# RWKV-7 attention and SwiGLU block on one core: the early triangular inverses of two chunks made together on 128 partitions

## The chip, the core and the metric

The kernel runs on one core of a Trainium2 chip. The metric is device time in microseconds from the first to the last work of one execution; the number given for a kernel is the median of several runs. Names of engines: PE is TensorE (matrix products and transposes), DVE is VectorE, ACT is ScalarE, POOL is GpSimd, SP is SyncE, which here only issues transfers (DMAs).

## The reference

Two layers stand one behind the other. The first is a linear recurrence over 768 time steps for 4 x 8 = 32 independent sequences with a 40 x 40 state each:

```
for t in range(S):
    y[:, :, t] = einsum('bhd,bhde->bhe', rt, state)
    Sa = einsum('bhde,bhe->bhd', state, at)
    state = state * wt[:, :, None, :] - einsum('bhd,bhe->bhde', Sa, bt) + einsum('bhd,bhe->bhde', vt, kt)
```

The second takes y as 3072 tokens of 320 numbers, divides each by its root mean square, and computes `(silu(xn @ w_gate) * (xn @ w_val)) @ w_out` with 1536 hidden units. All is float32; the weights arrive as 8-byte numbers whose halves the kernel reads as integers and narrows to float32 itself.

## The kernel before, in words

**Chunks.** The recurrence is cut into 24 chunks of 32 steps. For a chunk c there are four stages. `front(c)` loads w, a, k, b and v, transposes them on PE, and builds by levels 1, 2, 4, 8, 16 the matrix of the products between the steps of the chunk: on each level ACT copies an operand (`KE`), PE multiplies ("gram"), and DVE copies the masked product into the tile `LT`. The last of the five masked copies completes `LT`. `early_inverse(c)` (chunks 0 to 3) or `inverse(c)` (the others) solves the unit lower triangular system of each sequence. `main(c)` uses the inverse, the state and the products for the output y of the chunk and the next state, and turns y to tokens, normalized, in the tile `xg`. After every second chunk `feed(g)` runs the SwiGLU layer for the 256 tokens of two chunks: products of 256 columns with the gate and value weights (`xg,w` in the profile), and the product with `w_out` into PSUM tile `po`. `narrow(f, h)` makes the float32 weights; all 24 of these are due before feed 0 ends.

**The early inverse.** Each sequence's 32 x 32 triangle is split into two 16 x 16 diagonal blocks and one block between. The diagonal blocks of the 32 sequences lie on 64 partitions: partition u*32+n has block u of sequence n. To get there, four DMAs write `LT` to the DRAM tile `sB`, and two read it back into the part B of tile `M`. Then DVE does 15 steps of two instructions on the part Y of `M`: a product into `tmp`, and a subtraction from Y. Each needs the one before. ACT makes the negative transpose of the upper block (line 783), three DMAs write Y to the DRAM tile `sY`, and eight read it back, turned to the layout of PE, into the part E of `M`, which lies over the place of B and Y. PE then does two sets of 32 small products ("inv", lines 793 and 797), each copied out of PSUM by ACT, and the full inverse stands in E. `main(c)` uses it in the second set of its products "lower" (line 822, written `Xs,M` in the profile). Chunk c uses buffer c mod 2 of `M`.

**Order.** Nothing is scheduled at run time. The program first lists all pieces of work in a plan, and then issues them in the order of a written table `ORDER`: each number picks a piece relative to the first that is not yet issued, and a "-" puts in one filler product on PE (line 1010) that computes nothing needed. A second table, `PAIRS`, gives each PSUM tile its bank. Each engine works strictly in this order, SP's and POOL's transfers too: an instruction that waits holds up all that stands behind it on its engine. PE uses the products of the feeds as filling between the short, dependent products of the chunks.

Every helper records its engine's operation, so nearly all DVE work has line 453, PE 495 (products) and 498 (transposes), ACT 476 and 479, DMAs 492. Names in the rows: `LT_102`, `LT_103`, `LT_104` belong to chunks 0, 1 and 2, `M_135` and `M_136` are the two buffers of `M`.

## Time and profile before

| | |
|---|---|
| median of the runs | 932.68 us (three runs, 931.99 to 933.84) |
| time of the profiled execution | 934.37 us |
| its span, first to last instruction | 932.6 us |
| PE, DVE, ACT, POOL busy | 875.7, 723.2, 521.9, 294.9 us |
| mean granted clock of PE | 0.991 |

The page of the profile gives totals. A table by windows gives, for a stretch of the span, how long each engine was busy, the granted clock and the share of the DMA engines. A timeline gives single instructions with their start and duration in microseconds; in brackets stands the idle time of the engine before it, and what ended that.

### The profile page before, as it was taken

The page shows a single profiled execution, that of the slowest core. Times are in us where ns is not written, and L with a number is a line of the kernel's source. Part 1 is how long each engine was busy: PE and PEld are TensorE (multiplying, and loading weights), DVE is VectorE, ACT ScalarE, POOL GpSimd, SP SyncE. Part 2 cuts the span into 40 slices and gives each one's busy share as a digit, 9 for nine tenths or more (in the row PEclk, how much of TensorE's full clock was granted, in tenths as well). Part 3 has the DMA queues.
Part 4 walks back from the last instruction along what each step waited for, and adds up shares of the span by engine and source line. Part 5 has one row for each costly group of instructions (what it writes and reads, how often), then busy time and mean ns, then how long its engine had stood idle before and what let it go on. Part 6 is the DMA issues. An engine that isn't in the chain of part 4 may idle for free.

```text
span 932.6 us, 50195 instructions
## 1 busy us (share of the span) xinstructions
PE 875.7 (94%) x22072; PEld 703.2 (75%) x22072; DVE 723.2 (78%) x2702; ACT 521.9 (56%) x1144; POOL 294.9 (32%) x515
## 2 busy tenths in 40 slices
PE   4776898899999999999999999999999999999998
PEld 4665776677777788777777887887787777878776
DVE  5887778878878888978888888888888887864511
ACT  5887877674555566565555655655545454432211
POOL 8576546404221323432221333412503320200000
PEclk9999999899999999999999999999999999999999
DMA  9653546223242243333323223413414222021000
GB/s 162 104 119 84 126 98 153 73 69 67 55 87 49 46 86 73 71 59 60 70 39 74 64 54 75 89 35 71 88 21 85 61 41 62 11 60 28 3 15 15
DMA packets 146363, 63.01 MB, mean 68 GB/s; under 512 B 128800, under 2 KB 138080, under 8 KB 146144
## 3 DMA queue, kind: packets, MB, share of 16 engines
q1 hardware_dynamic: 125664, 29.46, 17.1%
q0 software_dynamic: 18368, 30.01, 15.1%
q8 instruction: 173, 2.83, 1.3%
q10 hardware_dynamic: 2112, 0.33, 0.3%
q14 instruction: 46, 0.38, 0.1%
HBM read 49.15 MB, written 10.09 MB: 64 GB/s over the span
## 4 chain that ended last, share of the span: by engine, by line
PE 72%; DMA 9%; DVE 6%; ACT 6%; issue 3%; SPq 2%; POOL 1%; DVEq 0%; POOLq 0%; ACTq 0%
PE ps L495 50%; PE po L495 14%; PE ps L498 7%; SPq L492 2%; DMA M<-sB 2%; DMA w<-in_moe_w_out_dram 1%; DMA LT<-sY 1%; DMA w<-in_moe_w_gate_dram 1%; DVE tmp L453 1%; DVE y L453 1%; DMA sY<-Yi 1%; ACT VU L476 1%; ACT KE L476 1%; DVE Yi L453 1%; DMA sY<-M 1%
## 5 line engine op out<-in xcount | busy, mean ns | idle before, releaser
L495 PE MATMUL ps<-xg,w 128*128 128x256 f32 (+1 forms) x1728 | 354.2, 393 | 1.2 <-DVE Yi L453 0.5
L495 PEld LDWEIGHTS ps<-xg,w 128*128 128x128 f32 (+1 forms) x1728 | 263.7, 191 | 49.1 <-issue 12.4
L495 PE MATMUL po<-w,hT 128*128 128x320 f32 x576 | 179.0, 449 | 0.0
L492 POOL DMA_DIRECT2D VU<-in_v_dram x184 | 102.4, 560 | 172.7 <-PE ps L495 78.1
L453 DVE TENSOR_TENSOR tmp<-Yi,M 128x60 f32<-128x60 f32 (+24 forms) x620 | 129.3, 209 | 20.5 <-DMA M<-sB 6.1
L453 DVE TENSOR_TENSOR Yi<-Yi,tmp 128x60 f32<-128x60 f32 (+24 forms) x620 | 129.7, 210 | 13.8
L473 ACT ACTIVATE sg<-ps 128x256 f32<-128x256 f32 x144 | 52.6, 384 | 150.6 <-PE ps L495 143.1
L495 PEld LDWEIGHTS po<-w,hT 128*128 128x128 f32 x576 | 106.0, 192 | 37.4 <-issue 1.9
L476 ACT COPY KE<-K 128x512 f32<-128x512 f32 x168 | 110.6, 662 | 26.2 <-DVE K L453 18.2
L453 DVE TENSOR_TENSOR hT<-ps,sg 128x256 f32<-128x256 f32 x144 | 58.3, 420 | 68.7 <-ACT sg L473 57.4
L453 DVE TENSOR_TENSOR K<-K,T 128x256 f32<-128x256 f32 x240 | 98.9, 421 | 10.2 <-ACT KE L476 8.8
L495 PE MATMUL ps<-A,KE 40*64 40x72 f32 x3840 | 95.0, 247 | 9.0 <-ACT KE L476 1.7
L495 PEld LDWEIGHTS ps<-A,KE 40*64 40x64 f32 x3840 | 79.2, 149 | 28.9 <-issue 9.3
L476 ACT COPY KN<-ps 128x320 f32<-128x320 f32 x144 | 67.4, 471 | 59.1 <-PE ps L495 28.5
L453 DVE COPY_PREDICATED LT<-msk,ps 128x256 f32<-128x256 uint32 x120 | 65.9, 550 | 19.5 <-PE ps L495 10.2
L482 POOL TENSOR_TENSOR ss<-ss,mhalf 128x1 f32<-128x1 f32 x24 | 15.4, 641 | 194.2 <-DVE ss L453 179.2
L453 DVE TENSOR_TENSOR y<-y,ps 128x256 f32<-128x256 f32 x119 | 49.9, 419 | 11.0 <-PE ps L495 7.9
L453 DVE TENSOR_TENSOR A<-A,T 128x128 f32<-128x128 f32 (+1 forms) x168 | 55.8, 335 | 1.5 <-ACT A L476 0.4
L495 PEld LDWEIGHTS ps<-As,KN 64*40 64x40 f32 x3840 | 45.1, 123 | 12.7 <-issue 4.4
L495 PE MATMUL ps<-As,KN 64*40 64x32 f32 x3840 | 50.3, 204 | 3.1 <-DVE y L453 1.6
L476 ACT COPY VU<-ps 32x320 f32<-32x320 f32 x96 | 40.0, 417 | 15.5 <-PE ps L495 14.2
L492 POOL DMA_DIRECT2D wan<-in_w_dram x44 | 29.1, 661 | 57.4 <-PE ps L498 57.1
(121 smaller groups left out, 1250.2 us busy)
## 6 DMA issues: line engine op xcount, KB each, us to landing
M<-sB SPq DMA_DIRECT2D x80, 128.0 KB, 3.4
rn<-in_r_dram SPq DMA_DIRECT2D x24, 160.0 KB, 4.6
out_dram<-o SPq DMA_DIRECT2D x48, 80.0 KB, 2.3
VU<-in_v_dram POOLq DMA_DIRECT2D x184, 20.0 KB, 2.6
kbn<-in_b_dram POOLq DMA_DIRECT2D x44, 80.0 KB, 3.4
kbn<-in_k_dram POOLq DMA_DIRECT2D x44, 80.0 KB, 3.3
wan<-in_w_dram POOLq DMA_DIRECT2D x44, 80.0 KB, 3.1
wan<-in_a_dram POOLq DMA_DIRECT2D x44, 80.0 KB, 3.3
```

The source lines that it names most:

```text
L453: plan.add("DVE", kind, lambda at: fn(at(o), *m(at)), [o], aps(*args))
L473: plan.add("ACT", "act", lambda at: nc.scalar.activation(at(o), at(a), f, **kw), [o] + aps(acc), [a])
L476: plan.add("ACT", "copy", lambda at: nc.scalar.copy(at(o), at(a)), [o], [a])
L482: plan.add("POOL", "tt", lambda at: nc.gpsimd.tensor_tensor(o, a, b, op), [o], [a, b])
L492: plan.add(by, "dma", lambda at: queue.dma_start(out=o, in_=i), [o], [i])
L495: return o, lhsT, rhs, lambda at: nc.tensor.matmul(at(o), lhsT, rhs, start=start, stop=stop, skip_group_check=True)
L498: return o, i, ident, lambda at: nc.tensor.transpose(at(o), i, ident)
```

## The change

`early_inverse` is called only at chunks 1 and 3 and works for two chunks. The diagonal blocks of both lie in the M tile of the even chunk, on all 128 partitions: partition (2u+q)*32+n has block u of sequence n of the pair's chunk q. The 30 DVE instructions per inverse keep their number of elements per partition; there are two sets of them and no longer four. What follows, from the DMAs to `sY` on, is still done per chunk, each chunk's E in its own tile `M`.

```
-        return (f[0:2 * BH, 0:h * h].rearrange("p (s t) -> p s t", s=h),
-                f[0:2 * BH, h * h:3 * h * h].rearrange("p (s t) -> p s t", s=h),
+        return (f[:, 0:h * h].rearrange("p (s t) -> p s t", s=h),
+                f[:, h * h:3 * h * h].rearrange("p (s t) -> p s t", s=h),
...
-                dma(halves(M)[0][u * BH:(u + 1) * BH], sB.rearrange("n (s t) -> n s t", s=C)[:, (1 - u) * HC:(2 - u) * HC, u * HC:(u + 1) * HC])
+                dma(halves(Z[c - c % 2]["M"])[0][(2 * u + c % 2) * BH:(2 * u + c % 2 + 1) * BH], sB.rearrange("n (s t) -> n s t", s=C)[:, (1 - u) * HC:(2 - u) * HC, u * HC:(u + 1) * HC])
...
     def early_inverse(c):
-        z = Z[c]
         plan.stage = "inverse", c
-        LT = z["LT"]
-        B, Y, E, A = halves(z["M"])
+        B, Y, _, _ = halves(Z[c - 1]["M"])
...
         for i in range(HC - 1):
             n, m = i + 1, HC - 1 - i
-            tmp = tmp_.next()[0:2 * BH, 0:n * m].rearrange("p (s t) -> p s t", s=n)
-            tt(tmp, Y[:, 0:n, m:m + 1].to_broadcast((2 * BH, n, m)), ap(B, m * HC + HC - 1, (0, n), (-1, m)), MUL)
+            tmp = tmp_.next()[:, 0:n * m].rearrange("p (s t) -> p s t", s=n)
+            tt(tmp, Y[:, 0:n, m:m + 1].to_broadcast((P, n, m)), ap(B, m * HC + HC - 1, (0, n), (-1, m)), MUL)
             tt(Y[:, 0:n, 0:m], Y[:, 0:n, 0:m], tmp, SUB)
-        scale(Y[0:BH, :, HC:], Y[0:BH, :, 0:HC].rearrange("p s t -> p t s"), -1.0)
-        sY = sY_.next()[:, 0:3 * HC * HC].rearrange("n (s t) -> n s t", s=HC)
-        dma(sY[:, :, 0:HC], Y[0:BH, :, 0:HC])
-        dma(sY[:, :, HC:C], Y[BH:2 * BH, :, 0:HC])
-        dma(sY[:, :, C:], Y[0:BH, :, HC:])
-        blank(E[:, :, 0:C], 0.0)
...
+        scale(Y[0:2 * BH, :, HC:], Y[0:2 * BH, :, 0:HC].rearrange("p s t -> p t s"), -1.0)
+        held = []
+        for q in range(2):
+            sY = sY_.next()[:, 0:3 * HC * HC].rearrange("n (s t) -> n s t", s=HC)
+            dma(sY[:, :, 0:HC], Y[q * BH:(q + 1) * BH, :, 0:HC])
+            dma(sY[:, :, HC:C], Y[(2 + q) * BH:(3 + q) * BH, :, 0:HC])
+            dma(sY[:, :, C:], Y[q * BH:(q + 1) * BH, :, HC:])
+            held.append(sY)
+        for q in range(2):
+            z, sY = Z[c - 1 + q], held[q]
+            LT = z["LT"]
+            _, _, E, A = halves(z["M"])
+            blank(E[:, :, 0:C], 0.0)
...
             front(c + 2)
-            (early_inverse if c + 2 < EARLY else inverse)(c + 2)
+            if c + 2 >= EARLY:
+                inverse(c + 2)
+            elif c % 2:
+                early_inverse(c + 2)
```

What follows in the second loop (eight loads of E, two sets of products, two copies) is as before. The tables `ORDER` and `PAIRS` are written anew throughout; one line of the old table and one of the new:

```
-0 225 226 223 0 0 0
...
+1211 1101 1207 1208 1209 1117 1116 1210 453 1066 1119 1394 1392 1146 1118 1067 454 1068 1069 1199 1070 1142 1120 1071
```

The number of PE's pieces (929) and of SP's transfers (486) stays; DVE's pieces go from 2699 to 2639, ACT's from 1122 to 1120, POOL's from 506 to 502, and the filler products on PE from 28 to 32. The last 146 pieces on PE and the last 479 on DVE stand in the same order in both.

Where the rows now stand, at three places. On DVE, around the inverse of chunk 0 (`tmp` and `M_135`) and the last masked copies of chunk 1 (`COPY_PREDICATED LT_103`), before:

```order
L453 TENSOR_TENSOR K_129<-K_129,T_126 128x16x16
L453 TENSOR_TENSOR tmp_139<-M_135 64x55
L453 COPY_PREDICATED LT_103<-msk,ps_65 128x32x8
L453 TENSOR_TENSOR M_135<-M_135,tmp_139 64x5x11
L453 TENSOR_TENSOR tmp_140<-M_135 64x60
L453 TENSOR_TENSOR K_129<-K_129,T_126 128x16x16
L453 TENSOR_TENSOR M_135<-M_135,tmp_140 64x6x10
L453 TENSOR_TENSOR tmp_139<-M_135 64x63
```

and now, at the first step of the inverse of chunks 0 and 1:

```order
L450 TENSOR_TENSOR T_127<-T_127 128x128
L450 TENSOR_TENSOR T_127<-T_127 128x64
L450 SCALAR_TENSOR_TENSOR w_154<-w_162,ex_171 128x480
L450 TENSOR_TENSOR tmp_139<-M_135 128x15
L450 TENSOR_TENSOR M_135<-M_135,tmp_139 128x15
L450 TENSOR_TENSOR tmp_140<-M_135 128x28
L450 TENSOR_TENSOR M_135<-M_135,tmp_140 128x2x14
L450 TENSOR_TENSOR tmp_139<-M_135 128x39
```

The inverse of chunk 0 ran between the last masked copies of chunk 1; the joint one begins after all of them, after three weight slices (`w_154` is written twice ahead of it) and after the first instructions of chunk 2 (`T_127`).

On SP, the transfers around the same inverses, before:

```order
L492 DMA sB1_174<-LT1_103 32x8x32 x3
L492 DMA gcol_84<-in_moe_rms_g_dram 128x1
L492 DMA sB1_174<-LT1_103 32x8x32
L492 DMA sY0_175<-M0_135 32x16x16 x3
L492 DMA M1_136<-sB1_174 32x16x16 x2
L492 DMA M0_135<-sY0_175 16x8x16 x4
L492 DMA M0_135<-sY0_175 16x8x32 x4
```

and now:

```order
L489 DMA sB1_174<-LT1_103 32x8x32 x4
L489 DMA M0_135<-sB1_174 32x16x16 x2
L489 DMA rn0_97<-in_r_dram 64x16x40
L489 DMA gcol_84<-in_moe_rms_g_dram 64x1
L489 DMA sY0_175<-M0_135 32x16x16 x2
L489 DMA sY1_176<-M0_135 32x16x16 x3
L489 DMA sY0_175<-M0_135 32x16x16
L489 DMA gcol_84<-in_moe_rms_g_dram 64x1
L489 DMA M0_135<-sY0_175 16x8x16 x4
L489 DMA M0_135<-sY0_175 16x8x32 x4
L489 DMA M1_136<-sY1_176 16x8x16 x2
```

The six stores of both chunks to `sY` now stand together, ahead of the loads of chunk 0's E; the loads of chunk 1's E follow directly.

On PE, from the turning of chunk 0's output (`ident,y_146`) to the use of chunk 1's inverse (`Xs_143,M_136`), before:

```order
L498 MATMUL ps_63<-ident,y_146 128x40 x8
L495 MATMUL ps_64<-ST_101,aP_134 32x40 x32
L495 MATMUL ps_64<-VU_99,LT_103 32x40 x32
L498 MATMUL ps_65<-ident,ST_101 104x40 x16
L495 MATMUL ps_64<-A_131,KE 64x72 x16
L495 MATMUL ps_65<-M_136,LT_103 16x16 x32
L495 MATMUL ps_65<-M_136 32x16 x32
L495 MATMUL ps_63<-Xs_143,M_136 32x40 x32
```

and now:

```order
L495 MATMUL ps_64<-ident,y_146 128x40 x8
L495 MATMUL ps_65<-ident,KE 128x40 x16
L492 MATMUL ps_63<-VU_99,LT_103 32x40 x32
L492 MATMUL ps_65<-A_132,KE 64x72 x16
L492 MATMUL ps_63<-A_131,KE 64x72 x16
L492 MATMUL ps_64<-M_136,LT_103 16x16 x32
L1016 MATMUL po<-ident 128x128
L492 MATMUL ps_64<-M_136 32x16 x32
L492 MATMUL ps_63<-A_132,KE 64x72 x16
L492 MATMUL ps_64<-Xs_143,M_136 32x40 x32
```

Chunk 1's inverse is still used behind the turning of chunk 0's output, now with three products of chunk 3 (`A,KE`), a transpose and a filler between.

101 lines of the change are left out of this document (49 added, 52 removed), and 330 rows, old and new, of the table ORDER.

## The prediction

> **What bounds the kernel now.** First the head of the page, for the whole span:
>
> ```profile
> span 932.6 us, 50195 instructions
> ...
> PE 875.7 (94%) x22072; PEld 703.2 (75%) x22072; DVE 723.2 (78%) x2702; ACT 521.9 (56%) x1144; POOL 294.9 (32%) x515
> ```
>
> PE is idle for 932.6 - 875.7 = 56.9 us. Where, shows the table by windows, cut where chunk 0's inverse is used (57), where feed 0 begins (112.4), where chunk 3 is done (206.2) and at three later places; the columns are the window, its length, and the busy time of PE, PEld, DVE, ACT and POOL, then the granted clock, DMA share and GB/s:
>
> ```profile
> 0.00:57.00 57.00, 37.27 (x890) 31.75 (x894) 42.69 (x146) 41.88 (x84) 39.84 (x86) 1.00 0.76 123
> 57.00:112.40 55.40, 39.87 (x1339) 35.22 (x1331) 43.59 (x138) 44.47 (x95) 33.26 (x60) 1.00 0.51 116
> 112.40:160.00 47.60, 44.23 (x1149) 34.76 (x1147) 39.19 (x124) 37.78 (x76) 27.18 (x46) 1.00 0.55 121
> 160.00:206.20 46.20, 41.49 (x1153) 32.67 (x1151) 37.02 (x131) 31.95 (x73) 16.39 (x28) 0.89 0.34 82
> 206.20:314.00 107.80, 103.91 (x2710) 82.64 (x2713) 89.47 (x357) 59.84 (x138) 30.59 (x51) 0.98 0.31 60
> 314.00:640.00 326.00, 321.69 (x8836) 257.04 (x8823) 283.16 (x1112) 186.91 (x412) 101.19 (x169) 0.99 0.34 66
> ```
>
> Idle time of PE: 19.7, 15.5, 3.4, 4.7, 3.9 and 4.3 us in turn, and the remaining 5.4 us after 640. Before 112.4 no feed can run: PE has only short products, each waiting for a copy on ACT, a step on DVE or a DMA. From then on the feeds fill the gaps, and time is PE's work plus what idle time is left. PE's work is not changed. So the change can gain only by idle time of PE, at most 8.1 us between 112.4 and 206.2 and a few after it; and it can lose what it puts ahead of feed 0. VectorE's own time counts only through these.
>
> **The change: the steps removed.** Two sets of 30 VectorE instructions go. The view of the tile M groups them (median in the middle), and the rows by shape show what twice the partitions cost:
>
> ```profile
> L453 DVE TENSOR_TENSOR tmp<-M x60: 151/201/452, 35.0 to 150.3; 64x15 f32<-64x15 f32 x8, 64x28 f32<-64x28 f32 x8, 64x39 f32<-64x39 f32 x8, 64x48 f32<-64x48 f32 x8
> L453 DVE TENSOR_TENSOR M<-M,tmp x60: 158/200/243, 35.2 to 150.8; 64x15 f32<-64x15 f32 x8, 64x28 f32<-64x28 f32 x8, 64x39 f32<-64x39 f32 x8, 64x48 f32<-64x48 f32 x8
> ...
> L453 DVE TENSOR_TENSOR tmp<-M 64x60 f32<-64x60 f32 x8 | 1.7, 210 | 0.1
> ...
> L453 DVE TENSOR_TENSOR tmp<-Yi,M 128x60 f32<-128x60 f32 x3 | 0.7, 219 | 0.1
> ```
>
> 210 against 219 ns for 60 elements on 64 and on 128 partitions: a joint step costs what a single one did, within 9 ns. Removed are 60 x 0.20 = 12 us of VectorE. None of it is a term of the sum by itself, since VectorE isn't the bound; it pays through B, C and D below. The two ACT and four POOL instructions that go are single pieces off the path. The four more fillers on PE stand where PE waits and are costed at nothing; without that cover they would cost 4 x 0.58 us = 2.3 us by the filler at 57.52 below.
>
> **A. Main 0 begins later.** The joint inverse needs the last masked copy of chunk 1. DVE's timeline before:
>
> ```profile
> 24.28 0.44 DVE L453 COPY_PREDICATED LT<-msk,ps 128x256 f32<-128x256 uint32 x1 [2.82 <-PE ps L495]
> ...
> 35.02 0.17 DVE L453 TENSOR_TENSOR tmp<-M 64x15 f32<-64x15 f32 x1 [0.49 <-DMA M<-sB]
> ...
> 39.44 0.22 DVE L453 TENSOR_TENSOR M<-M,tmp 64x64 f32<-64x64 f32 x1
> 39.58 0.42 DVE L453 COPY_PREDICATED LT<-msk,ps 128x256 f32<-128x256 uint32 x1
> 39.91 0.21 DVE L453 TENSOR_TENSOR tmp<-M 64x63 f32<-64x63 f32 x1
> ...
> 42.94 0.18 DVE L453 TENSOR_TENSOR M<-M,tmp 64x15 f32<-64x15 f32 x1
> ```
>
> and SP's queue with PE's use of the result:
>
> ```profile
> 40.08 1.30 SPq L492 DMA_DIRECT2D sB<-LT  x3
> 41.42 1.19 SPq L492 DMA_DIRECT2D gcol<-in_moe_rms_g_dram  x1
> 42.65 0.43 SPq L492 DMA_DIRECT2D sB<-LT  x1
> 43.19 1.48 SPq L492 DMA_DIRECT2D sY<-M  x3
> 45.15 0.83 SPq L492 DMA_DIRECT2D M<-sB  x2
> ...
> M<-sB SPq DMA_DIRECT2D x80, 128.0 KB, 3.4
> ...
> 56.30 1.29 PE L495 MATMUL ps<-Xs,M 32*32 32x40 f32 x64
> 57.52 0.58 PE L1010 MATMUL po<-ident 128*128 128x128 f32 x1
> ```
>
> - Chunk 1's last copy ended at 40.00 behind 16 steps of inverse 0 (35.02 to 39.44). Without them: 40.0 - 16 x 0.20 = 36.8.
> - From the last copy to the first step, two DMA hops: chunk 0 took 35.02 - 24.72 = 10.3 us. The lower bound is from chunk 1's rows without the two foreign transfers in its queue: four issues (1.30 + 0.43), 45.15 - 43.08 = 2.1 to landing, 0.83 for two issues and 3.4 to landing make 8.1. In the new order nothing stands between; I take 9.2, the middle: first step at 46.0. Three weight slices and chunk 2's first instructions on DVE stand in this gap and cost nothing.
> - 30 steps at the pace of the 14 from 39.91 to 43.12, 0.23 us: 6.9 us, end at 52.9.
> - From the last step to the use on PE it took 56.30 - 43.12 = 13.2 us. Six stores to sY now stand ahead of the loads in place of three, 1.5 us more by the row of three; the last store waits for ACT's transpose anyway, so 1.0. Use at 67.1.
>
> So the first use of chunk 0's inverse goes from 56.3 to 67.1: **+10.8 us** (bounds: 8.1 and 0 give +8.5, 10.3 and 1.5 give +12.4). Behind this wait stand on PE all of main 0, and on SP the first stores of chunk 2, which is not yet needed.
>
> **B. Main 1 waits less.** PE around chunk 1's inverse before, the steps of inverses 1 and 2 that stood between main 0's instructions on DVE (six; first and last), and the first product of feed 0:
>
> ```profile
> 75.32 0.65 PE L498 MATMUL ps<-ident,y 40*128 40x40 f32 x8 [1.64 <-DVE y L453]
> ...
> 82.00 0.68 PE L495 MATMUL ps<-M,LT 32*16 32x16 f32 x58 [0.52 <-DMA M<-sY]
> 85.41 1.12 PE L495 MATMUL ps<-M 16*32 16x16 f32 x64 [2.73 <-ACT M L476]
> 86.90 1.29 PE L495 MATMUL ps<-Xs,M 32*32 32x40 f32 x64 [0.36 <-ACT M L476]
> ...
> 112.39 2.08 PE L495 MATMUL ps<-xg,w 64*128 64x256 f32 x8
> ...
> 68.17 0.16 DVE L453 TENSOR_TENSOR tmp<-M 64x15 f32<-64x15 f32 x1
> ...
> 71.34 0.18 DVE L453 TENSOR_TENSOR M<-M,tmp 64x28 f32<-64x28 f32 x1
> ```
>
> Inverse 1 was the last to come (its loads ended a wait at 82.00). Now it is done with inverse 0, while main 0 still runs. The waits 0.52 + 2.73 + 0.36 = 3.6 us and six steps of 0.16 us = 1.0 can go: **-4.6 us**. If ACT's copy is as late again, only 0.52 + 1.0 = 1.5 go. If chunk 1 also gains from the work that ran between 75.97 and 82.00, about 6. The rest of the chain from here to 112.39 has the same pieces in both orders. Feed 0 begins 10.8 - 4.6 = 6.2 us later, at 118.6.
>
> **C. Chunks 2 and 3 beside feed 0.** Inverse 3 came late before; its stores and loads on SP, the use, and the first product of feed 1:
>
> ```profile
> 151.02 2.79 SPq L492 DMA_DIRECT2D sY<-M  x3
> 157.64 4.37 SPq L492 DMA_DIRECT2D M<-sY  x8
> ...
> 171.70 0.69 PE L495 MATMUL ps<-Xs,M 32*32 32x40 f32 x54
> ...
> 207.86 0.92 PE L495 MATMUL ps<-xg,w 64*128 64x256 f32 x6
> ```
>
> Main 3 could use its inverse only at 171.70, so xg for feed 1 came just ahead of 207.86, and PE was idle for 3.4 + 4.7 = 8.1 us in this stretch. In the new order the joint inverse of 2 and 3 ends near feed 0's first product, so main 3 waits only for main 2, and VectorE has some 6 us less to do here. If PE then idles as it does from 314 to 640 (4.3 of 326 us, 1.3%), 93.8 us keep 1.2: **-6.9 us**. Bounds: half, -3.5, if the other waits (states, weights, copies) set it; -8.1, if all goes.
>
> **D. After chunk 3.** From 206.2 to 314 PE idles 3.9 us. At 1.3%, 1.4 would be left: **-2.5 us** (0 to -3.9). Later the order differs little, and the end is the same.
>
> **The sum**: 10.8 - 4.6 - 6.9 - 2.5 = -3.2 us. The profiled execution took 934.37 us, 932.6 in its span and 1.8 around it; so it would be 931.2. It lies 1.7 us above the median of the runs, 932.68, for which the forecast is **929.5 us**, faster by 0.3%.
>
> **Rivals.** What a measurement can tell from no change is 0.2%, 1.9 us.
>
> 1. Slower: the wait for the second chunk isn't made good. The place is main 0: if A stands at its upper bound (12.4), and B gives only 1.5, feed 0 begins 10.9 us later; if then C gives half (3.5) and D half (1.2), it is 932.7 + 6.2 = 938.9. It decides as soon as A less B is above C plus D, here 9.4 us. For it: A is a chain of DMAs, each measured, with no cover. Against: B's waits are in the trace as well.
> 2. No change: VectorE's 12 us were mostly hidden. C and D at 70% of the above, 6.6 us, against 6.2: 932.3. For it: DVE is busy 39.19 of 47.60 us, not all, and ACT 37.78.
> 3. More: A at +8.5, B at -6, C at -8.1, D at -3.9 makes 923.2. For it: the whole order was made anew and moves other waits too. Against: it needs every bound at once.
> 4. The clock. Rows of 20 us each:
>
> ```profile
> 20.00:40.00 20.00, 14.77 (x278) 12.10 (x270) 14.43 (x51) 14.28 (x31) 12.30 (x23) 1.00 0.73 123
> 160.00:180.00 20.00, 16.68 (x500) 12.96 (x498) 17.02 (x63) 14.06 (x32) 8.42 (x15) 0.95 0.28 68
> 180.00:200.00 20.00, 18.65 (x466) 15.13 (x463) 15.04 (x52) 12.45 (x25) 6.02 (x11) 0.79 0.40 101
> ```
>
> The granted clock fell once in this part, costing 20 x (0.05 + 0.21) = 5.2 us of full clock, where PE was well filled, and not at 20 to 40 where it idled most. If PE's longer wait for main 0 makes it fall once more, the forecast becomes 929.5 + 5.2 = 934.7. The Trainium skill, "TensorE: Matmul & The Clock Gate", section "What's actually happening", says that the gate halves the clock after an idle window of about 3.4 us; by that rule this change would invite it, and the trace doesn't agree so far, since the fall stands in filled time.
>
> The change can't fail to do what it says: the two sets of steps are gone from the program.
>
> **How the numbers follow.** The forecast as summed has 0.36, the greater gain 0.10, no change 0.22, the slow case 0.28, the clock 0.04. Faster: 0.46; within 0.2%: 0.22; slower: 0.32. The likeliest case's own range is 926.7 to 930.8 (a gain of 1.9 to 6). The range that should hold the time 8 times in 10 takes in rival 3 and most of rival 1: 922 to 938.
>
> **What would show it.** A: the first step of the first joint inverse at 46 and its first use on PE near 67; earlier than 63 makes A wrong. B: 26 us between the uses of the inverses of chunks 0 and 1 on PE, where it was 86.90 - 56.30 = 30.6; over 29 makes B wrong. Feed 0's first product at 117 to 121. C: use of inverse 3 no longer behind its loads, and under 4 us of idle PE between feed 0's start and the end of main 3. D: under 2 us idle in the next 108. If feed 0 begins no later than 113 and the time is still not lower, the idle time after it was not VectorE's, and C is wrong; if feed 0 begins after 122, rival 1 is at work.

## The result, and the profile after

| | before | after |
|---|---|---|
| median of the runs | 932.34 us (4 runs) | 942.33 us (4 runs, 940.53 to 942.91) |
| ratio, 95% interval | | 1.0102 (1.0072 to 1.0133) |
| time and span of the profiled execution | 934.37, 932.6 us | 940.53, 938.8 us |

The changed kernel is slower by 1.0%, 9.5 us by the ratio (6.7 to 12.4). The forecast was 929.5 us, with a range of 922 to 938. The same kernel, run again on another chip (label g3), gave 943.16 against 932.33 us, 1.0112 (1.0073 to 1.0150), as expected there:

> The changed kernel itself once more, beside the others on one chip, to put its loss on the same footing as theirs: 940 to 944 us by the first comparison (1.0072 to 1.0133 of before). If it comes out at 936 to 938 here, a third of the loss first measured was chance between chips, and the parts found so far would explain it without a rest.

The two profiled executions differ by only 6.2 us: that of before lay 2.0 us above its median in this comparison, that of after 1.8 below. So the traces show about two thirds of the loss. The head of the page of after, and its table by windows with the columns of the prediction:

```profile
span 938.8 us, 50107 instructions
...
PE 877.7 (93%) x22080; PEld 705.0 (75%) x22080; DVE 716.6 (76%) x2642; ACT 520.3 (55%) x1142; POOL 293.0 (31%) x511
```

```profile
0.00:57.00 57.00, 32.16 (x656) 27.28 (x656) 41.57 (x131) 43.55 (x84) 38.90 (x86) 0.86 0.67 129
57.00:112.40 55.40, 37.81 (x1362) 33.10 (x1364) 36.79 (x93) 41.91 (x87) 32.76 (x56) 0.50 0.51 116
112.40:160.00 47.60, 45.53 (x1133) 35.68 (x1129) 32.92 (x99) 32.45 (x73) 21.92 (x37) 0.85 0.44 99
160.00:206.20 46.20, 42.03 (x1159) 33.90 (x1160) 38.59 (x142) 30.36 (x68) 20.50 (x34) 0.93 0.39 91
206.20:314.00 107.80, 105.82 (x2831) 84.61 (x2830) 89.57 (x351) 63.95 (x146) 32.65 (x55) 0.98 0.31 64
314.00:640.00 326.00, 320.61 (x8688) 256.06 (x8674) 284.11 (x1113) 186.59 (x410) 99.04 (x165) 1.00 0.32 63
```

Idle time of PE in turn: 24.8, 17.6, 2.1, 4.2, 2.0 and 5.4 us, and 5.0 after 640; before it was 19.7, 15.5, 3.4, 4.7, 3.9, 4.3 and 5.4. Up to 112.4 that is 7.2 us more, from there to 314 3.7 us less, later 0.7 more: 4.2 us in all. PE's busy time rose by 2.0, with four fillers more. VectorE's busy time fell by only 6.6 us (723.2 to 716.6) for the 60 instructions that the prediction had put at 12 us.

The joint steps on DVE in after's timeline, with chunk 1's last masked copy ahead, two steps of chunk 2 behind, and chunk 2's last masked copy; then ACT's copy for chunk 2's second gram:

```profile
33.26 0.44 DVE L450 COPY_PREDICATED LT<-msk,ps 128x256 f32<-128x256 uint32 x1 [0.82 <-PE ps L492]
...
41.37 0.16 DVE L450 TENSOR_TENSOR tmp<-M 128x15 f32<-128x15 f32 x1
...
48.56 0.18 DVE L450 TENSOR_TENSOR M<-M,tmp 128x15 f32<-128x15 f32 x1
48.85 0.42 DVE L450 TENSOR_TENSOR K<-K,T 128x256 f32<-128x256 f32 x1
...
49.70 0.46 DVE L450 TENSOR_TENSOR K<-K,T 128x256 f32<-128x256 f32 x1
...
73.98 0.44 DVE L450 COPY_PREDICATED LT<-msk,ps 128x256 f32<-128x256 uint32 x1
...
50.20 0.67 ACT L473 COPY KE<-K 128x512 f32<-128x512 f32 x1
```

and PE of after, from chunk 2's second gram to the use of chunk 0's inverse (63.65), the turning of chunk 0's output (82.08), the use of chunk 1's inverse (94.81), and the first products of feeds 0 and 1:

```profile
50.92 1.24 PE L492 MATMUL ps<-A,KE 40*64 40x72 f32 x32 [6.59 <-ACT KE L473]
...
63.65 0.87 PE L492 MATMUL ps<-Xs,M 32*32 32x40 f32 x34 [0.96 <-ACT M L473]
...
82.08 0.65 PE L495 MATMUL ps<-ident,y 40*128 40x40 f32 x8 [1.79 <-DVE y L450]
85.49 1.24 PE L492 MATMUL ps<-A,KE 40*64 40x72 f32 x32 [0.69 <-ACT KE L473]
87.93 1.24 PE L492 MATMUL ps<-A,KE 40*64 40x72 f32 x32 [1.21 <-ACT KE L473]
89.10 0.72 PE L492 MATMUL ps<-M,LT 32*16 32x16 f32 x64
...
91.39 1.05 PE L492 MATMUL ps<-M 16*32 16x16 f32 x64 [0.84 <-ACT M L473]
...
94.81 1.29 PE L492 MATMUL ps<-Xs,M 32*32 32x40 f32 x64 [1.20 <-ACT M L473]
...
121.53 2.80 PE L492 MATMUL ps<-xg,w 64*128 64x256 f32 x9
...
211.67 1.08 PE L492 MATMUL ps<-xg,w 64*128 64x256 f32 x8
```

Set against the rows of before:

| start on PE, us | before | after | difference |
|---|---|---|---|
| use of chunk 0's inverse | 56.30 | 63.65 | +7.35 |
| use of chunk 1's inverse | 86.90 | 94.81 | +7.9 |
| feed 0 | 112.39 | 121.53 | +9.1 |
| feed 1 | 207.86 | 211.67 | +3.8 |
| end of the span | 932.6 | 938.8 | +6.2 |

Three things are to be seen. The inverse of chunk 0 is late, as forecast, though less. The 30 joint steps stand in a row on DVE, with only one other short instruction between them (at 45.30), and chunk 2's next steps stand behind it (48.85, 49.70); chunk 2's gram on PE waits 6.59 us for an ACT copy (50.20) that begins when the second of these has ended. And from the use of inverse 0 to feed 0 nothing is won back: the use of inverse 1 comes 7.9 us later and feed 0 9.1.

### The profile page after: what moved, and what is told of

The parts are those of the page before. It is cut to its first block, busy times and chain, and to the rows that moved or that the text cites. A ratio compares the mean times of both kernels' runs of the same rounds, so it can differ in the third digit from the quotient of the medians.

```text
span 938.8 us, 50107 instructions
## 1 busy us (share of the span) xinstructions
PE 877.7 (93%) x22080; PEld 705.0 (75%) x22080; DVE 716.6 (76%) x2642; ACT 520.3 (55%) x1142; POOL 293.0 (31%) x511
## 3 DMA queue, kind: packets, MB, share of 16 engines
q1 hardware_dynamic: 125664, 29.46, 16.7%
## 4 chain that ended last, share of the span: by engine, by line
PE 78%; ACT 6%; DVE 5%; DMA 4%; issue 4%; POOL 2%; SPq 1%; DVEq 0%; ACTq 0%; POOLq 0%
PE ps L492 54%; PE po L492 15%; PE ps L495 8%; ACT VU L473 2%; SPq L489 1%; DVE y L450 1%; DMA LT<-sY 1%; ACT KE L473 1%; DVE LT L450 1%; DMA sY<-Yi 1%; DVE K L450 1%; ACT KN L473 1%; DVE tmp L450 1%; DMA kbn<-in_b_dram 1%; ACT sg L470 1%
## 5 line engine op out<-in xcount | busy, mean ns | idle before, releaser
L492 PE MATMUL ps<-A,KE 40*64 40x72 f32 x3840 | 95.5, 246 | 17.2 <-ACT KE L473 9.5
L492 PEld LDWEIGHTS ps<-A,KE 40*64 40x64 f32 x3840 | 79.1, 148 | 39.7 <-ACT KE L473 14.9
L450 DVE TENSOR_TENSOR y<-y,ps 128x256 f32<-128x256 f32 x119 | 50.0, 420 | 12.8 <-PE ps L492 10.1
L492 PE MATMUL ps<-As,KN 64*40 64x32 f32 x3840 | 53.1, 206 | 5.3 <-ACT y L473 2.0
```

What stands on the lines that cost most here:

```text
L450: plan.add("DVE", kind, lambda at: fn(at(o), *m(at)), [o], aps(*args))
L492: return o, lhsT, rhs, lambda at: nc.tensor.matmul(at(o), lhsT, rhs, start=start, stop=stop, skip_group_check=True)
```

## The experiments

Fifteen edits beside the repeat. "Use 0", "feed 0" and so on are starts on PE as in the table. A time in us behind a ratio is the ratio less one, times the median of before in the same comparison.

### What VectorE's freed time is worth: e1

Before's order, without the steps of the inverses of chunks 1 and 3; all that stands around them stays.

```
-        for i in range(HC - 1):
+        for i in range(0 if cs[0] in (1, 3) else HC - 1):
```

> The kernel before, with its order, but the 30 VectorE steps of the inverses of chunks 1 and 3 are left out (60 instructions, their chunks' inverses stay blank, so the values are wrong from chunk 1 on; everything else runs as before). It has the VectorE time that the joint steps save (60 x 0.21 = 12.6 us) with no delay of chunk 0. Theory 'delay' (the joint steps lose because chunk 0's inverse comes later, while the freed VectorE time is worth about what the prediction's terms B, C and D said, 4.6 + 6.9 + 2.5 = 14.0 us): 918 to 922 us. Rival 'hidden' (VectorE's time there lies beside other work, so freeing it gives little in any order): 930 to 933 us.

928.39 against 934.39 us (8 and 20 runs), ratio 0.9942 (0.9918 to 0.9965): 5.4 us less. That is between the two expectations and nearer to the rival's. VectorE's freed time has a worth without any other edit, but half or less of what the durations of 60 steps add up to. Feed 0 came at 111.5, 0.9 earlier. In this order, at least, the removed steps are worth no more: here they are gone altogether, with no inverse made later.

### What a later main 0 costs: e3, g2, g1

e3 makes each multiplication of chunk 0's inverse three times; the result is the same.

```
-            tt(tmp, Y[:, 0:n, m:m + 1].to_broadcast(...), ..., MUL)
+            for _ in range(3 if cs[0] == 0 else 1):
+                tt(tmp, Y[:, 0:n, m:m + 1].to_broadcast(...), ..., MUL)
```

> The kernel before, with its order, but each multiplication of inverse 0 is made three times over (30 more VectorE instructions of 0.21 us, the values stay the same): inverse 0 comes some 6.3 us later and nothing is saved or moved. Theory 'delay': PE first uses inverse 0 at 62 to 63 us instead of 56.3, feed 0 begins 5 to 7 us later, and the whole program is 5 to 8 us longer: 937 to 940 us. Rival 'slack' (a delay of main 0 is made good by feed 0, and the change lost its time elsewhere): 932 to 934 us.

938.21 us (9 runs), 1.0058 (1.0032 to 1.0084): 5.4 us. Use 0 and feed 0 were both 5.8 us later. But the added steps also hold VectorE. g2 makes the same inverse late without VectorE: its result goes twice more through device memory.

```
+            if cs[0] == 0:
+                for a, b in ((sZ, sY), (sY, sZ)):
+                    dma(a[:, :, :], b[:, :, :])
```

> The kernel before with all its work and its order; the result of inverse 0 is copied twice more through device memory before it is loaded, so that main 0 gets it some 5 to 6 us later while VectorE loses nothing and chunk 2's front keeps its place. Theory 'inverse 0' (main 0 later, feed 0 later, end later): use of inverse 0 at 61 to 63, feed 0 4 to 6 us later, 935 to 938 us, as with the late inverse 0 made by VectorE. Rival 'VectorE' (in that earlier run the 30 added VectorE instructions cost the time, not the later inverse): 931 to 934.

SP's timeline in g2 shows the two detours ahead of the loads:

```profile
46.82 0.55 SPq L495 DMA_DIRECT2D sZ<-sY  x1
49.97 0.49 SPq L495 DMA_DIRECT2D sY<-sZ  x1
52.28 3.62 SPq L495 DMA_DIRECT2D M<-sY  x8
```

936.24 against 932.33 us (6 and 11 runs), 1.0042 (1.0021 to 1.0064): 3.9 us, for a use 3.6 later (59.9) and a feed 0 4.2 later. The delay alone costs about what it is long; nothing behind it makes it good.

g1 tests the other cause, the row. Nothing is added or removed: the 30 steps of chunk 1's inverse, which before spread between other work, stand in one row at the place of the first.

```
  ORDER: the 30 pieces tmp<-M, M<-M,tmp of chunk 1's inverse
-   between other pieces, from the first one's place on
+   all at the first one's place, one behind the other
```

> The kernel before with single inverses and all its work; on VectorE the 30 steps of inverse 1 (from 49.0 to 69.7 us, between other work) stand in one row at their first place, so that chunk 2's front waits behind them on VectorE as it does behind the joint row of the change; inverse 0 and the loads of its result stay where they were, and inverse 1 is ready earlier. Nothing else moves. Theory 'row' (a row of 30 dependent steps holds chunk 2's front, whose gram products stand ahead of main 0 in PE's queue): chunk 2's last mask at 61 to 64 instead of 56.9, use of inverse 0 at 59 to 62 instead of 56.3 though its operands are there in time, feed 0 3 to 5 us later, and 935 to 938 us. Rival 'inverse 0 alone' (only the later inverse 0 cost the change time): use of inverse 0 at 56 to 57.5, and 930 to 933.

DVE, SP and PE of g1, first and last step of the row with the next step of chunk 2 (56.78); the loads of chunk 0's E; ACT's copy for chunk 2's gram; that gram (58.22) and what follows up to the use:

```profile
49.89 0.18 DVE L456 TENSOR_TENSOR tmp<-M 64x15 f32<-64x15 f32 x1 [0.93 <-DMA M<-sB]
...
56.69 0.18 DVE L456 TENSOR_TENSOR M<-M,tmp 64x15 f32<-64x15 f32 x1
56.78 0.41 DVE L456 TENSOR_TENSOR K<-K,T 128x256 f32<-128x256 f32 x1
```

```profile
47.94 4.07 SPq L495 DMA_DIRECT2D M<-sY  x8
```

```profile
57.22 0.62 ACT L479 COPY KE<-K 128x512 f32<-128x512 f32 x1 [7.87 <-DVE K L456]
```

```profile
58.22 1.24 PE L498 MATMUL ps<-A,KE 40*64 40x72 f32 x32 [8.39 <-ACT KN L479]
59.39 0.73 PE L498 MATMUL ps<-M,LT 32*16 32x16 f32 x64
...
63.30 1.29 PE L498 MATMUL ps<-Xs,M 32*32 32x40 f32 x64
```

937.97 us (6 runs), 1.0074 (1.0043 to 1.0106): 6.9 us. Chunk 0's E was loaded in time (the loads were issued by 52.0 and landed by 53.4), yet use 0 came 7.0 us later. PE's next instruction was chunk 2's gram. It waited 8.39 us for copies on ACT, ACT waited 7.87 us for a step of chunk 2 that stood behind the row on VectorE, and the products with E stand behind the gram in PE's queue. So a row of dependent steps for one chunk delays another chunk's inverse that is ready. This is the clearest of the runs: same work, another order on one engine.

### Which part of the change does it: f1, f2, f3, f4

f1 and f2 are the changed kernel without the joint steps of one pair, everything else in its place.

```
-        for i in range(HC - 1):
+        for i in range(0 if cs[-1] == 1 else HC - 1):        (f1; in f2: == 3)
```

> The changed kernel, with its order, but the 30 joint steps of chunks 0 and 1 are left out (their inverses stay blank, the rest runs). Main 0 can then start when the last mask of chunk 1 is stored and loaded back, some 7 us earlier, and VectorE does not hold up chunk 2's front for 7.2 us. Theory 'delay' (what comes later before main 0 comes out later at the end, at 0.65 to 0.95 of itself as in the run with the late inverse 0): first use of inverse 0 at 56 to 57 us instead of 63.65, feed 0 at 114 to 116 instead of 121.5, and the time 934 to 938, level with the kernel before or a little behind it. Rival 'new order' (the loss lies behind main 0, in the order and in the pair 2-3): 939 to 943, as the change.

> The changed kernel, with its order, but the 30 joint steps of chunks 2 and 3 are left out (their inverses stay blank). Theory 'delay' (of the pair 0-1 alone; behind feed 0 PE has feed products that cover a late inverse 2): the use of inverse 2 moves from 141.5 to 132 to 136 us, but the time only to 938 to 942. Rival 'pair 2-3' (the second pair's late inverse costs as much as the first's): use of inverse 2 at 130 to 134, feed 1 6 to 9 us earlier, and 932 to 936 us.

f1: 939.65 against 931.76 us (10 and 13 runs), 1.0077 (1.0051 to 1.0103). Even with all 30 steps gone, use 0 is only 2.3 us earlier than in after (61.3), so the expectation of 56 to 57 was wrong. ACT and PE of f1 show why:

```profile
47.33 0.72 ACT L472 ACTIVATE o<-w,ctop 128x480 f32<-128x480 int16 x1 [0.58 <-DMA w<-in_moe_w_val_dram]
47.96 0.65 ACT L478 ACTIVATE M<-M 64x256 f32<-64x256 f32 x1
...
49.10 0.66 ACT L475 COPY KE<-K 128x512 f32<-128x512 f32 x1
```

```profile
49.81 1.24 PE L494 MATMUL ps<-A,KE 40*64 40x72 f32 x32 [5.43 <-ACT KE L475]
```

The next thing in line was late as well. On ACT a weight slice waits for its load (47.33), and behind it stand the inverse's transpose (`M<-M`) and chunk 2's `KE`. PE idles 5.43 of the 6.59 us all the same. In this order the row and the weight slice hold up the same work at the same time, so taking away one brings little. That also makes the run a poor measure of the row alone. Feed 0 came at 117.5, 4.0 us earlier than in after; so of its 9.1 us of delay 5.1 are there without any joint step of this pair, and the time was still 7.2 us (4.8 to 9.6) above that of before.

f2: 942.37 us (4 runs), 1.0105 (1.0071 to 1.0139). Removing the 30 steps of the pair 2 and 3 altogether gains nothing that can be measured; the use of chunk 2's inverse came 1.7 us earlier (139.8), where 132 to 136 was expected. These steps cost the changed order nothing that can be seen in its time.

f3 keeps all work of after and breaks up the row of the pair 0 and 1: behind every fourth step stands one of seven other pieces, six of chunk 2's front and one of a weight slice.

```
  ORDER: row of 30 joint steps of chunks 0 and 1
+   after every 4th step one piece of front(2) or narrow
```

> The changed kernel with all its work, but the 30 joint steps of chunks 0 and 1 no longer stand in one row on VectorE: behind every fourth of them stands one instruction of chunk 2's front (or of a weight's narrowing) that stood behind the whole row. Theory 'delay' (main 0 sets the end, chunk 2's front has slack): inverse 0 comes 1 to 4 us later still, PE's idle stretch of 6.59 us at 44.33 shrinks, and the time is 943 to 947. Rival 'block' (what cost time is that the row of steps held up chunk 2's front and left PE idle for 6.6 us): feed 0 earlier than 121.5 and 934 to 939 us.

944.32 us (4 runs), 1.0125 (1.0092 to 1.0157). PE of f3:

```profile
50.00 1.24 PE L496 MATMUL ps<-A,KE 40*64 40x72 f32 x32 [5.11 <-ACT KE L477]
```

Chunk 2's gram waits 1.5 us less, and chunk 0's inverse comes 1.4 us later (65.1); feed 0 begins at 123.5. Mixed in this way the row only changes the loser: what chunk 2 gains, main 0 pays.

f4 is the other half of the change alone: before's order, with only chunks 2 and 3 joint, in one row from 112.35 on.

```
+JOINT = (3,)
...
+            elif (c + 2) | 1 not in JOINT:
+                early_inverse([c + 2])
```

> The kernel before, in its own order, with chunks 2 and 3 joint and nothing else changed: the steps of inverse 2 (on VectorE from 70.5 to 97.6 us) are gone, and the 30 joint ones stand in one row where inverse 3's began (112.7). It repeats the run with the pair 2-3 alone without that run's seam between two orders, which put three weight slices and their waits ahead of feed 0. Theory 'delay' with cover by feed 0: inverse 2 is used at 135 to 139 us instead of 131.4, feed 0 stays at 112.4, and the time is 931 to 935. Rival 'pair 2-3': inverse 2 at 139 to 142, feed 1 7 to 10 us later, 938 to 943 us.

945.07 us (4 runs), 1.0135 (1.0083 to 1.0188). Feed 0 began as before (112.1), but the use of chunk 2's inverse went from 131.4 to 143.9 and feed 1 from 207.9 to 222.6. PE of f4:

```profile
128.38 0.23 PE L497 MATMUL ps<-M,LT 32*16 32x16 f32 x4 [4.94 <-DMA M<-sY]
...
134.90 2.20 PE L497 MATMUL ps<-A,KE 40*64 40x72 f32 x64 [4.44 <-DVE hT L455]
```

This is the side of the rival, and more than it said. Chunk 2's inverse is now made only where chunk 3's was; then the feed's `hT` stands on VectorE behind a weight slice that waits 5.85 us for ACT. These are two idle stretches of PE, 9.4 us, in a place where PE idled 3.4 us in 47.6 before. In after the use of chunk 2's inverse comes 20.0 us behind feed 0 (141.5), against 19.1 before: measured from feed 0 the pair costs little there.

An earlier attempt at the same, e2, took before's order up to feed 0 and the change's behind it.

```
+JOINT = (3,)
  ORDER: pieces up to feed 0 as before, from there as in the change
```

> Only the inverses of chunks 2 and 3 are made together; 0 and 1 stay single. Up to the first product of feed 0 the order is that of the kernel before (without the steps of inverse 2), from there on that of the change. Theory 'delay': all of the loss came from the pair 0-1, so chunk 0's inverse is used at 56.3 us as before and feed 0 begins at 112.4 or a little earlier, and the time is 926 to 932 us. Rival 'new order' (the loss was in the order found anew after feed 0, or in the pair 2-3, whose inverse comes later): 936 to 942 us, with feed 0 at 112.4 all the same. Rival 'hidden': 932 to 934 us.

985.15 us (6 runs), 1.0536 (1.0496 to 1.0576). At the seam three weight slices came ahead of feed 0, which began at 127.3, so the run tells nothing about the pair.

### Why main 1 gained nothing: h1, h2

Two edits of the changed kernel's order, with nothing else changed. h1 puts chunk 1's inverse (its loads, its two products and their copies) and its first use ahead of what stood between of chunk 3's front, but for one gram.

```
  ORDER, PE from the turning of chunk 0's output (y) to the use (Xs,M); A,KE are chunk 3's:
-   y   A,KE   A,KE   M,LT   M   A,KE   Xs,M
+   M,LT   y   M   A,KE   Xs,M   A,KE   A,KE
```

> The changed kernel with all its work; only the order differs: the loads, the two sets of products and the two copies of chunk 1's inverse, and its first use by main 1, stand ahead of the pieces of chunk 3's front that stood between them on PE and ACT. Theory (the prediction's gain for main 1 was lost because, between the turning of chunk 0's output at 82.1 us and the use of chunk 1's inverse at 94.8, PE and ACT wait for chunk 3's front): the use falls to 88 to 91 us, feed 0 from 121.5 to 117 to 119, and the time from 942.3 to 937 to 940. Rival (that place is not the bound; what main 1 gains there it waits for later, in its own chain or for chunk 3): the use falls as well, but feed 0 stays at 120.5 to 123 and the time at 941 to 945.

943.84 against 934.85 us (4 and 7 runs), 1.0108 (1.0075 to 1.0141). PE of h1, the first product with chunk 1's E, its use, and the longest wait behind it:

```profile
82.55 0.72 PE L495 MATMUL ps<-M,LT 32*16 32x16 f32 x64 [1.81 <-DVE y L453]
...
89.92 1.29 PE L495 MATMUL ps<-Xs,M 32*32 32x40 f32 x64 [0.32 <-ACT Xs L479]
...
98.20 0.92 PE L498 MATMUL ps<-ident,ST 40*104 40x40 f32 x16 [2.77 <-ACT KN L476]
```

Chunk 1's inverse is used 4.9 us earlier than in after (94.81), and feed 0 begins 1.7 later, at 123.3. The rival holds. The turning of chunk 0's output, now behind the first product with E, came 1.7 us later as well (83.74), and from there to feed 0 it is 39.5 us as in after, though the use stands 6.2 us behind the turning and no longer 12.7. The wait for inverse 1 can be taken out, and then PE waits elsewhere: 2.77 us for ACT's copies of chunk 3's front (`KN`) at a place where after waits 0.45.

h2 asks for the other suspect. In after the last level of chunk 2's front, whose gram stood ahead of the use of chunk 0's inverse before (55.13), stands behind main 0's first products, and its masked copy ends at 74.4 where it ended at 56.9. h2 puts it directly behind that use.

```
  ORDER: the last gram of chunk 2 with its operand, masked copy and copy
-   behind main 0's products VU,KN and rE,vut
+   directly behind the use of chunk 0's inverse
```

> The changed kernel with all its work; only the order differs: the last gram of chunk 2 with its operand, masked copy and copy stands directly behind the use of chunk 0's inverse, where in the change it stands behind main 0's next products. Theory (chunk 2's late last copy, at 74.4 us, holds up the loads of chunk 1's inverse and chunk 3's front, and so main 1): the last copy ends at 66 to 69 us, the use of chunk 1's inverse comes 2 to 3 us earlier, feed 0 at 118 to 120, time 938 to 941. Rival (nothing that main 1 needs waits for that copy last; the gram in front only holds up main 0): the last copy is earlier as well, but the turning of chunk 0's output and feed 0 come 1 to 4 us later, time 943 to 947.

945.79 us (4 runs), 1.0143 (1.0107 to 1.0179). DVE and PE of h2, the masked copy and the turning of chunk 0's output:

```profile
66.82 0.42 DVE L453 COPY_PREDICATED LT<-msk,ps 128x256 f32<-128x256 uint32 x1 [7.14 <-PE ps L495]
```

```profile
86.37 0.65 PE L498 MATMUL ps<-ident,y 40*128 40x40 f32 x8 [1.90 <-DVE y L453]
```

The copy ended 7.2 us earlier, but the turning came 4.3 us later and feed 0 at 125.8: DVE waited 7.14 us for this gram, with weight slices and main 0's steps queued behind. Again the rival. Main 1 doesn't wait for that copy.

### Is it the order, or the half clock at the start: e5 to e7, e4

e5 (four single inverses), e6 (both pairs) and e7 (only the pair 0 and 1) have the first 1500 pieces of the order searched anew, all three in one way.

```
+JOINT = ()        (e5; in e6 (1, 3), in e7 (1,))
  ORDER: the first 1500 numbers written anew
```

> All four early inverses single, as in the kernel before, but the order of the first 1500 pieces was searched anew, by moving one piece at a time ahead of or behind its neighbours on its engine and keeping what shortens the program when it is laid out with the durations and latencies that the profile of before shows. It is the partner of the next two runs: the same search was made for each of them. Theory 'pairing' (the change loses because joint inverses come later, in whatever order): this order is the fastest of the three, 910 to 930 us, with chunk 0's inverse used on PE at 50 to 56 us. Rival 'order' (the change lost because its order was worse, not because of the joint steps): the three come out within 3 us of each other. If the layout leaves out what decides, this run is no faster than 934.

> Both pairs joint, as in the change, with the order of its first 1500 pieces searched anew in the same way and with as many trials as the run before this one. Theory 'pairing': faster than the change's 942, but 6 to 12 us behind the searched order with single inverses, with the first use of chunk 0's inverse 6 to 7 us later there than in that run and feed 0 4 to 7 us later. Rival 'order': level with the single inverses to 3 us, or ahead of them, since 60 VectorE instructions fewer must help once the order is right.

> Only chunks 0 and 1 joint; 2 and 3 single; order of the first 1500 pieces searched anew in the same way. Theory 'pairing of 0-1 makes the delay': the first use of chunk 0's inverse comes as late as with both pairs (6 to 7 us behind the single ones), and chunk 2's inverse is used earlier than with both pairs by 4 to 6 us, so the time lies between the two other runs, 2 to 6 us ahead of both pairs joint. Rival 'order': all three within 3 us.

962.54, 965.64 and 979.13 against 932.55 us: 1.0316 (1.0278 to 1.0354), 1.0349 (1.0299 to 1.0398) and 1.0488 (1.0447 to 1.0529). e5 and e6 lie 3 us apart, but e7, which is between them in content, lies 15 us behind. The scatter of the search is larger than the difference that was sought: inconclusive. What remains is that an order can cost 30 to 45 us with the same work, several times what the change is about.

e4 is before with 118 more fillers on PE ahead of feed 0, to see whether the low clock at the start sets its length.

```
  ORDER: 14 "-" ahead of PE's first product, 104 in gaps up to feed 0
```

> The kernel before, with its order, and 118 more of its filler products on PE before feed 0: 14 ahead of the first product, the others in the gaps that PE had in the profile of before, each gap filled to 0.8 by fillers of 0.215 us, which is what one takes at the full clock. Theory 'half clock' (TensorE runs at half its clock until feed 0, since no stretch without a gap is long enough to raise it and keep it; gram products take 1.24 us there and 0.73 us at the full clock): the clock is up before 20 us, gram products of chunks 0 to 3 take 0.73 us, feed 0 begins 5 to 15 us earlier, and the time is 918 to 928 us. Rival 'latency' (the chain before feed 0 is one of waits on ACT, DVE and transfers, so faster products give nothing, and fillers only delay): 932 to 940 us. If the clock does not rise, the fillers take 0.42 us each and the time is 945 to 960 us.

948.24 us (6 runs), 1.0173 (1.0141 to 1.0206). PE of e4:

```profile
28.44 0.73 PE L500 MATMUL ps<-A,KE 40*64 40x72 f32 x32
```

A gram took 0.73 us where before's took 1.24, so the clock did rise; but use 0 came only 1.1 us earlier and feed 0 1.5 us later. The clock didn't stay up: its records say 0.50 from 48.8 to 62.5 and from 69.3 to 79.5. In that part twenty products of fillers took 4.63 us ahead of main 0's next step, where twenty took 2.50 us at 10.56, and from use 0 to the turning it was 24.6 us, 5.5 more than before. From the turning to feed 0, for the most part at 1.00, it was 34.1 us, 2.9 less than before, fillers included. So the run shows that these fillers gain nothing in sum; what a full clock alone would bring, it doesn't show. Behind feed 1 it lost a further 10 us, and there PE stands eight times, 9.9 us in all, waiting for nothing that the profile shows (once, 1.4 us, in before). Why isn't known.

## Why the prediction was wrong

**The account by steps.** The table of starts and the sum of the prediction have the same cuts:

| step | predicted | measured |
|---|---|---|
| A, use 0 | +10.8 | +7.35 |
| B, from there to feed 0 | -4.6 | +1.8 |
| C, feed 0 to feed 1 | -6.9 | -5.3 |
| D and all that follows | -2.5 | +2.4 |
| span | -3.2 | +6.2 |

The measured span lies 9.4 us above the forecast one. B makes 6.4 of that, D 4.9 and C 1.6; A was milder than forecast by 3.4 and hides as much, which is luck.

**A** had the right mechanism and was mis-sized, below its lower bound of 8.5 (its own terms add up to 8.7). Chunk 1's last copy ended at 33.70 and not at 36.8, since the new order also moved its front ahead. The two hops then took 7.7 us (bounds 8.1 and 10.3), the 30 steps 7.4 (6.9), and from the last step to the use it was 14.9 us (14.2). The mark "earlier than 63" wasn't passed, but the first step at 46 was wrong: 41.37. In g3's trace use 0 comes at 64.93, 8.6 us late, and yet the turning of chunk 0's output (82.00) and feed 0 (121.45) stand within 0.1 us of the first trace. So in this order 1.3 us more at use 0 don't move feed 0.

**B** is the step that failed. 31.2 us lie between the uses of the inverses of chunks 0 and 1, where 26 were predicted and over 29 was to make it wrong. The windows from use 0 to feed 0, before and after (length, then PE's busy time):

```profile
56.30:112.39 56.09, 40.56 (x1370) 35.91 (x1366) 44.15 (x139) 45.11 (x96) 33.95 (x61) 1.00 0.50 116
```

```profile
63.65:121.53 57.88, 42.81 (x1426) 37.60 (x1426) 40.28 (x114) 44.97 (x93) 30.09 (x53) 0.50 0.43 100
```

Divided at the turning of chunk 0's output and at use 1, with the measured change split into PE's busy and idle time:

| | predicted | measured | busy | idle |
|---|---|---|---|---|
| use 0 to turning (before 19.0 us) | -1.0 | -0.6 | -1.1 | +0.5 |
| turning to use 1 (before 11.6 us) | -3.6 | +1.2 | +2.0 | -0.8 |
| use 1 to feed 0 (before 25.5 us) | 0 | +1.2 | +1.4 | -0.2 |
| together | -4.6 | +1.8 | +2.2 | -0.5 |

The prediction took 4.6 us off this stretch, most of it idle time of PE. Only 0.5 us of idle time went, and 2.2 us of PE's own work came in. Two things were wrong in it.

First, the waits for inverse 1. It put down all of 0.52 + 2.73 + 0.36 us. The 0.52 us for its transfers are gone, but the other 3.09 us ended on ACT's copies of the products with E, and 2.04 of these came back (0.84 and 1.20), much as the prediction's own bound had it ("if ACT's copy is as late again"). With the waits for the copies of chunk 3's grams (0.69 and 1.21, where one of 1.16 stood before) PE still idles 3.9 us from the turning to use 1, where it idled 4.8.

Second, what stands in between. From the turning to use 1 one gram of 32 products stood before, and three stand there now, all of chunk 3 (85.49, 87.93, 92.37). The two more are some 2.4 us of PE's work at 1.2 us each. The sum put them at nothing, though the new order, printed ahead of it, shows them. Chunk 3's front, whose first gram stood at 72.47 before, now begins at 85.49, in the midst of main 1, and shares ACT, DVE and PE with it. From use 1 to feed 0 PE's pieces are the same, as the prediction said, but for one transposition of the state (`ident,ST`), which stood ahead of use 1 before; PE idles 5.6 us there before and 5.4 now. So the terms that failed are the 3.6 us for the waits, of which 0.8 came, and the pieces of chunk 3 put ahead of use 1, which cost about 2 and had no term.

The length of this stretch goes with the order. From the turning to feed 0 it is 39.2 to 39.5 us in all seven traces of the changed order (after, g3, f1, f2, f3, h1, h2), and 36.8 to 37.5 in the six that keep before's order there (before, e1, e3, f4, g1, g2). Taking out joint steps (f1, f2) or the wait for inverse 1 (h1) doesn't alter it. So of feed 0's 9.1 us 6.8 are the turning's delay (75.32 to 82.08), and 2.4 are what the new order puts behind it.

What the prediction also left out is what the joint row does to others. It put the row down as 6.9 us of main 0's wait and never asked who else stood behind it on VectorE. Chunk 2's first four masked copies begin 4.0 to 5.9 us later than before (the first at 49.19, was 45.19), and its last one stands behind main 0. g1 shows what a row of this length costs by itself in before's order: 7.0 us at feed 0 and 6.9 us at the end, with an inverse 0 that is ready in time.

**C** came out by the starts (95.5 to 90.1 us between the feeds), but not by its mechanism. PE's idle time between the feeds fell by 2.4 us (8.1 to 5.6; 4.0 in g3's trace), where 6.9 were forecast, and the mark of under 4 failed in the first trace. The other 2.9 us are work that is done elsewhere: PE's busy time between the feeds fell from 87.4 to 84.5 us, and behind feed 1 it rose from 711.2 to 714.7. That is **D**'s +2.4: its idle time did fall, by 1.1 us to the end, and its mark held (2.0 us in the 108 after 206.2), but 3.5 us more work stands there. What C and D brought in time is read from the medians:

| | feed 0 later by, us | time longer by, us |
|---|---|---|
| g2, inverse 0 late by transfers | 4.2 | 3.9 (2.0 to 6.0) |
| e3, inverse 0 late by steps | 5.8 | 5.4 (3.0 to 7.8) |
| g1, a row for inverse 1 | 7.0 | 6.9 (4.0 to 9.9) |
| the change | 9.1 | 9.5 (6.7 to 12.4) |
| h1, the change with inverse 1 first | 10.9 | 10.1 (7.0 to 13.2) |
| f3, the change with the row mixed | 11.1 | 11.6 (8.6 to 14.6) |
| h2, the change with chunk 2's last level first | 13.4 | 13.4 (10.0 to 16.7) |

In the first three nothing was taken from VectorE, and a late feed 0 costs about its whole delay. The change and its variants lie on the same line. So what its freed VectorE time and its new order did after feed 0 left nothing in sum, as far as intervals of some 3 us to each side tell; by the single traces 2.9 us came back in after and 1.6 in g3. f2 agrees (no gain from 30 steps less), and e1 says that in before's order the freed time would have been worth 5.4 us. That the prediction let 9.4 us come back by C and D was thus the second error: it took idle time of PE as VectorE's doing, though no row showed these waits ending on VectorE's steps.

**VectorE's 12 us** were summed from recorded durations, and these overlap with those of the other instructions between which the single steps stood; the busy time fell by 6.6. The prediction said that they are no term by themselves, yet C used "some 6 us less to do".

**The fillers** were costed at nothing. With PE's busy time up by 2.0 and its idle time up too, the traces don't tell what they cost: a filler in a wait turns idle time into busy time.

**The rivals.** Rival 1 had the right side and the right place: "the wait for the second chunk isn't made good". Its mark was feed 0 after 122, and it was 121.53; its price of 6.2 us is just what the profiled executions differ by, but its time of 938.9 lies 3.4 us under the median. The match is in part luck, as it let A cost 12.4, B give 1.5 and C and D bring 4.7 back. It was given 0.28. Rival 4's argument, that the clock didn't fall where PE idles most, was no measurement, as the next section but one shows. The clock isn't what made the time, though: the start ran at half clock in both kernels, and from feed 0 on before has more of it (4.2 us up to its first record, then 10.2, 3.4 and 3.4) than after (5.3, 6.8 and 3.4 us).

**What stays open.** The 6.8 us by which the turning is late can't be divided into the row, the late inverse 0 and the late front of chunk 2: f1, f3 and h2 show that they hide one another. Whether an order exists in which the pair doesn't lose stays open too, as e5 to e7 don't tell. Where the further 3.8 us are lost by which the medians differ more than the profiled executions wasn't found. No version of the pair was found that beats before; e1 is faster because it leaves work out.

## What to carry to other kernels

When two jobs are joined so that each instruction does double work, the joint job starts with the later input and ends as one block: price the delay of the earlier user, and then list what stands behind the block on its engine, and behind those waits on every other engine's queue. A wait that ends last is worth only the distance to the next thing that would end last there. If the order is written anew, count the pieces on the stretch that decides, in both orders, before taking them as the same. In a start like this one, a chain of short dependent pieces, a delay cost about its whole length (g1, g2, e3), while freed time on an engine that wasn't the bound was worth a part of its sum (e1) or nothing (f2).

## What was unexpected in the hardware

**VectorE's durations overlap, unless a step needs the one before.** From 41.37 to 48.56 the joint steps take 7.19 us for 29 intervals, 0.248 us each, at recorded durations near 0.21: each begins some 0.03 us behind the end of the last. Independent ones of after begin before the last has ended:

```profile
51.24 0.28 DVE L450 TENSOR_TENSOR A<-A,T 128x128 f32<-128x128 f32 x1
51.45 0.41 DVE L450 TENSOR_SCALAR w<-w 128x480 int32<-128x480 int32 x1
51.76 0.42 DVE L450 TENSOR_TENSOR K<-K,T 128x256 f32<-128x256 f32 x1
```

(0.07 and 0.10 us before). The Trainium skill, "Perfetto Trace Analysis", section "Optimizing Scalar/DVE Operations", says that the latency in a profile is longer than the engine is busy, since its last part overlaps with the next instruction. These rows agree; that the overlap is lost in a chain of dependent steps is what the joint rows add.

**A clock of 1.00 in the table can mean that there is no record of it.** Before feed 0 a gram of 32 products takes 1.24 us in both kernels; in before it still does at 55.13, where the table gives 1.00, and is 0.73 at 128.98:

```profile
55.13 1.24 PE L495 MATMUL ps<-A,KE 40*64 40x72 f32 x32 [0.53 <-ACT A L476]
...
128.98 0.73 PE L495 MATMUL ps<-A,KE 40*64 40x72 f32 x32
```

So the start ran at half clock before, too. In after the records begin at 38.0, with one window of 3.4 us at 1.00, and then say 0.50 up to 126.8; in before they begin at 116.6. The gap between the mean clocks, 0.991 and 0.949, is mostly this.

**The clock also fell behind windows in which PE was half busy.** Windows of after, then of before; 38.0 to 41.4, 191.6 to 195.0 and 174.6 to 178.0 are the last ahead of a fall:

```profile
38.00:41.40 3.40, 0.04 (x2) 0.00 (x0) 3.37 (x9) 3.38 (x9) 1.74 (x3) 1.00 0.61 86
191.60:195.00 3.40, 1.72 (x73) 1.45 (x73) 1.71 (x5) 2.11 (x4) 0.27 (x1) 1.00 0.56 84
195.00:201.80 6.80, 5.70 (x136) 5.03 (x138) 4.80 (x15) 3.57 (x8) 0.00 (x0) 0.50 0.45 151
```

```profile
174.60:178.00 3.40, 1.85 (x101) 1.56 (x104) 3.10 (x13) 3.13 (x7) 0.41 (x1) 1.00 0.02 6
```

The first agrees with the rule that the prediction took from the Trainium skill, "TensorE: Matmul & The Clock Gate", section "What's actually happening": an idle window of about 3.4 us ends the full clock. The other two don't: PE was busy 1.72 and 1.85 of the 3.40 us, and the clock fell all the same. In g2 it fell at 136.2 behind a window with PE busy for 2.63 us.
